# Forty-two unread matmuls in the waits of TensorE at the start of an attention and feed-forward kernel

## The chip, the core and the metric

The kernel runs on one core of one Trainium2 chip. The core has five engines that run their own queues of instructions: TensorE (PE in the profile, with its weight loads as PEld), VectorE (DVE), ScalarE (ACT), GpSimd (POOL) and SyncE (SP, which here only issues transfers). The metric is the device time of one execution in microseconds (us); less is better. The kernel before took 344.17 us, the median of three runs from 341.67 to 345.38 us.

## The reference

Eight batches of eight heads of causal attention, 576 queries each, with 16 beacon keys that every query may see; the result, as 4608 rows of 512, goes through a feed-forward layer of width 2048 with an ELU between its two products.

```python
k_all = np.concatenate([beacon_k, k], axis=2)          # B=8, H=8, S=576, D=64, 16 beacons
v_all = np.concatenate([beacon_v, v], axis=2)
scores = scale * np.matmul(q, k_all.transpose(0, 1, 3, 2))
scores = np.where(causal, -1000000000.0, scores)
a = np.exp(scores - scores.max(-1, keepdims=True)); a /= a.sum(-1, keepdims=True) + 1e-09
x = np.matmul(a, v_all)                                # -> (4608, 512)
h = x @ w_in                                           # (512, 2048)
g = np.where(h > 0.0, h, np.exp(np.minimum(h, 0.0)) - 1.0)
out = g @ w_out                                        # (2048, 512)
```

## The kernel before

The work is cut into pairs of heads: pair `n` is two heads of batch `n // 4`. For a pair of the first three batches, q and k are loaded as 32-bit floats (L261, issued by SP or ACT), cast to 16 bits (`cast_pair`, L215 when on DVE), and turned by nine plus one transposes on TensorE. For the four pairs of the first batch that is `do_T2` (L355 to L364): its ten transposes fill two tiles named `tr2`, and four copies (`do_copy2`) on ACT and DVE bring them to `kT` and `qT`. For later batches `do_T` (L351, L353) uses one tile of another kind. From batch 3 on, transfers do the turning.

`do_SC` (L402) then makes the scores of a pair in four units, each in a tile of kind `sc`, of which there are two. ACT takes the exponential of each (`do_exp`, L411), POOL zeroes what the causal mask forbids (`do_mask`, L418), and `do_AV` (L438) multiplies by v (loaded, then cast by L215) into a tile `av`. DVE divides by the row sums (L453, L454), and for the first two batches `do_xT` (L464) turns the result, which ACT or DVE copies to `xT` (L213, L215). The feed-forward layer follows by tiles of rows: the first product into `hps` (L494), the exponential on ACT (L501), a clamp on POOL (L505), the join on DVE (L512), and the second product (L569, and L561 in a form with fewer products).

The order of the work is written out by hand. Every operation has a number in `KEYS`, `plan.run` sorts all operations by it and issues them in that order, and each engine executes its own in the order issued. There are no priorities at run time: an instruction whose inputs are not ready holds up all that stand behind it on its engine.

A list `FILLS` has numbers of the same kind. For each, `plan.run` issues one call of `do_fill` (L200 to L203) at the place that the number gives in the order: a matmul of a tile of ones by itself, 128 by 256, into a tile `spare` that nothing reads. Before, there are 29 at 7.543 and two at 9.623. They stand in TensorE's queue ahead of the first pair's transposes, and between the first and the second pair's.

A tile `spare` is not a place of its own:

```python
            spare = psum.tile([P, 512], FP32, tag="ff", name="spare", bufs=4)
            nc.tensor.matmul(out=spare[:, 0:2 * P], lhsT=ones[:, 0:P], rhs=ones, start=True, stop=True)
```

`tag="ff"` with `bufs=4` is a ring of four banks of PSUM that go round in the order in which tiles are asked for, and `tr2` (two of the four for each pair), `av`, `xt` and `hps` come from the same ring. The k-th tile of the ring takes the bank of the (k-4)-th. So the matmul that writes it waits until all that wrote or read the (k-4)-th tile is done, the copies on ACT and DVE too. The list of operations keeps count of the ring for all its own work (`take=["ff"]`, `give=["ff"]`), not for `do_fill`.

Of the kernel before, what the change touches and what calls it, by code (L numbers as in the profile page):

```python
# [58 lines left out]
def kernel(  # L59
# [131 lines left out]
    with tc.tile_pool(name="psum", bufs=1, space=bass.MemoryType.PSUM) as psum:  # L191
# [406 lines left out]
        def do_store(s, m, halves):  # L598
# [11 lines left out]
        FILLS = [  # L610
            7.543, 7.543, 7.543, 7.543, 7.543, 7.543, 7.543, 7.543, 7.543, 7.543, 7.543, 7.543, 7.543, 7.543, 7.543,
            7.543, 7.543, 7.543, 7.543, 7.543, 7.543, 7.543, 7.543, 7.543, 7.543, 7.543, 7.543, 7.543, 7.543, 9.623,
            9.623,
        ]
        KEYS = [
# [483 lines left out]
```

## Time and profile before

| | |
|---|---|
| runs, median (lowest to highest) | 344.17 us (341.67 to 345.38) |
| the profiled execution's own time | 343.9 us |
| its span, first to last instruction | 342.2 us |
| TensorE busy | 326.2 us, 95% of the span |
| DVE, ACT, POOL busy | 240.5, 222.4, 191.6 us |
| transfers | 52.59 MB in 139399 packets |
| granted TensorE clock, mean | 0.989 |

The profile is of one execution. Its times count from the start of the span; the time of the execution is 1.7 us longer than the span. "Busy" of TensorE is the time with a matmul under way, which says nothing of its speed: that is in the granted clock (PEclk), 1.00 for full. In lists of instructions a row gives the start, the duration of the whole row, the engine, the line, what is written from what, and how many instructions were merged (x8); in brackets stands the idle time of the engine before it and what ended it.

### The profile page before, as it was taken

What the parts mean: (1) busy time and instruction counts of PE and PEld (TensorE: products, weight loads), DVE (VectorE), ACT (ScalarE), POOL (GpSimd) and SP (SyncE); (2) the same over time, 40 slices, a digit from 0 to 9 for tenths busy, and PEclk for the clock granted to TensorE, in tenths of its full rate; (3) what the DMA queues carried; (4) which work ended last, traced back from release to release, by engine and by line L of the source; (5) the groups of instructions that cost most, each with busy time, mean ns of one, the idle gap of its engine ahead of it and who ended that gap; (6) DMA issues with size and microseconds to landing.
All of it is one profiled execution on the core that took longest, in us unless ns stands there. A gap on an engine that the chain in (4) does not pass through costs nothing.

```text
span 342.2 us, 9215 instructions
## 1 busy us (share of the span) xinstructions
PE 326.2 (95%) x3615; PEld 225.8 (66%) x3615; DVE 240.5 (70%) x467; ACT 222.4 (65%) x347; POOL 191.6 (56%) x358
## 2 busy tenths in 40 slices
PE   7578999999999998999999999999999999999994
PEld 5356888645635674577687876675667676666684
DVE  1878879565788786766767678567776776694762
ACT  2867897877588656875577768867764663344420
POOL 4575799377658853457457475655562645434400
PEclk9969999999999999999999999999999999999999
DMA  7989999899979999999899899965604200500113
GB/s 228 250 230 243 261 244 211 162 173 186 181 145 202 213 208 152 194 203 207 152 151 227 154 140 186 214 161 123 135 0 103 62 2 12 153 32 33 61 48 108
DMA packets 139399, 52.59 MB, mean 154 GB/s; under 512 B 119388, under 2 KB 135772, under 8 KB 139356
## 3 DMA queue, kind: packets, MB, share of 16 engines
q1 hardware_dynamic: 114492, 42.11, 58.9%
q10 hardware_dynamic: 20640, 5.70, 10.3%
q0 software_dynamic: 4224, 4.19, 7.5%
q8 instruction: 28, 0.46, 0.6%
q14 instruction: 15, 0.12, 0.1%
HBM read 37.22 MB, written 9.44 MB: 136 GB/s over the span
## 4 chain that ended last, share of the span: by engine, by line
PE 75%; DMA 7%; DVE 7%; ACT 5%; POOL 2%; issue 2%; SPq 1%; ACTq 0%; DVEq 0%
PE hps L494 31%; PE ops L561 26%; PE av L438 7%; PE sc L402 7%; DMA kT<-st 4%; PE ops L569 3%; ACT et L411 3%; DVE gt L512 2%; DMA st<-in_q_dram 2%; DMA vst<-in_v_dram 2%; DVE st L215 1%; POOL e L505 1%; DVE v L215 1%; PE tr L351 1%; ACT e L501 1%
## 5 line engine op out<-in xcount | busy, mean ns | idle before, releaser
L505 POOL TENSOR_SCALAR e<-e 128x512 f32<-128x512 f32 x144 | 93.3, 654 | 94.9 <-ACT e L501 94.1
L494 PE MATMUL hps<-xT,w_in 128*128 128x512 f16 (+2 forms) x768 | 140.9, 326 | 0.7 <-DVE gt L512 0.5
L411 ACT ACTIVATE et<-sc 128x1024 f16<-128x1024 f32 (+4 forms) x128 | 109.7, 891 | 32.6 <-PE sc L402 26.7
L512 DVE SCALAR_TENSOR_TENSOR gt<-e,hps 128x512 f16<-128x512 f32 x144 | 96.3, 681 | 48.8 <-POOL e L505 48.5
L501 ACT ACTIVATE e<-hps 128x512 f32<-128x512 f32 x144 | 84.2, 600 | 48.8 <-PE hps L494 45.9
L494 PEld LDWEIGHTS <-w_in 128*128 128x128 f16 x768 | 66.0, 98 | 46.5 <-issue 5.8
L418 POOL TENSOR_SCALAR_AFFINE_SELECT et<-et 128x256 f16<-128x256 f16 (+4 forms) x160 | 69.6, 457 | 27.7 <-ACT et L411 27.4
L561 PEld LDWEIGHTS <-gt 128*128 128x128 f16 x640 | 60.9, 98 | 14.2 <-issue 1.4
L561 PE MATMUL ops<-w_out,gt 128*128 128x256 f16 x384 | 47.1, 273 | 0.0
L402 PE MATMUL sc<-qT,kT 64*128 64x80 bf16 (+3 forms) x704 | 37.7, 235 | 5.2 <-ACT et L411 2.7
L438 PEld LDWEIGHTS <-et 128*128 128x128 f16 (+1 forms) x992 | 37.4, 99 | 7.5 <-issue 1.6
L438 PE MATMUL av<-v,et 128*128 128x65 f16 (+1 forms) x992 | 40.7, 196 | 1.3 <-DVE v L215 1.3
L402 PEld LDWEIGHTS <-kT 64*128 64x128 bf16 x704 | 21.1, 97 | 23.5 <-issue 17.5
L454 DVE TENSOR_TENSOR x<-av,rl 128x256 f16<-128x256 f32 (+2 forms) x68 | 32.0, 471 | 2.5 <-DVE rl L453 0.2
L561 PE MATMUL ops<-t,gt 128*128 128x256 f16 x256 | 31.6, 273 | 0.0
L561 PEld LDWEIGHTS <-s 128*128 128x128 f16 x256 | 24.4, 98 | 5.6 <-issue 0.6
L453 DVE RECIPROCAL rl<-av 128x4 f32<-128x4 f32 (+2 forms) x68 | 12.3, 182 | 17.0 <-PE av L438 16.9
L594 DVE TENSOR_TENSOR osb<-ops,part 128x512 f32<-128x512 f32 (+1 forms) x27 | 16.9, 628 | 9.7 <-PE ops L561 6.0
L215 DVE CAST st<-st 128x1152 bf16<-128x1152 f32 (+3 forms) x19 | 15.7, 827 | 8.2 <-DMA st<-in_k_dram 3.4
L213 ACT ACTIVATE part<-ops 128x512 f32<-128x512 f32 (+1 forms) x22 | 12.2, 560 | 12.1 <-PE ops L561 12.0
L561 PE MATMUL ops<-t,s 128*128 128x256 f16 x128 | 16.1, 273 | 0.0
L569 PE MATMUL ops<-w_out,gt 128*128 128x512 f16 x64 | 16.0, 379 | 0.0
(54 smaller groups left out, 207.3 us busy)
## 6 DMA issues: line engine op xcount, KB each, us to landing
out_dram<-osb SPq DMA_DIRECT2D x32, 256.0 KB, 2.5
vst<-in_v_dram SPq DMA_DIRECT2D x18, 256.0 KB, 5.8
st<-in_q_dram SPq DMA_DIRECT2D x16, 256.0 KB, 4.4
st<-in_q_dram SPq DMA_DIRECT2D x11, 288.0 KB, 6.5
st<-in_k_dram SPq DMA_DIRECT2D x11, 288.0 KB, 6.5
st<-in_k_dram SPq DMA_DIRECT2D x9, 256.0 KB, 4.9
w_in<-in_moe_w_in_dram POOLq DMA_DIRECT2D x4, 512.0 KB, 9.6
w_out<-in_moe_w_out_dram POOLq DMA_DIRECT2D x4, 512.0 KB, 8.7
```

What stands on the lines that cost most here:

```text
L215: eng.tensor_copy(out=out, in_=in_)
L402: nc.tensor.matmul(out=sc[:, h, o:o + w], lhsT=kT[D * h:D * h + D, keys_of(n, jc)], rhs=qT[D * h:D * h + D, q0:q0 + w], start=True, stop=T ...
L411: nc.scalar.activation(out=et[:, :, 0:w], in_=scs[n, u][:, :, 0:w], func=AFT.Exp, bias=0.0, scale=float(1.0 / (D ** 0.5)))
L418: nc.gpsimd.affine_select(out=et[:, :, c0:c0 + dw], in_=et[:, :, c0:c0 + dw], compare_op=ALU.is_ge, fill=fill0, base=q0 + NB - keys.start, ...
L438: nc.tensor.matmul(out=av[:, c:c + D + 1], lhsT=ets[n, cut.unit_of[jc, at]][0:m, h, col:col + P], rhs=v16[0:m, jc, 2 * hp + h, 0:D + 1], s ...
L454: nc.vector.tensor_tensor(out=x16s[b % 2][:, blks[0]:blks[0] + nb, P * hp:P * hp + P].rearrange("q i (h d) -> q i h d", d=D), in0=av[:, :, ...
L494: nc.tensor.matmul(out=hps[:, (hi - lo) * j + a - lo:(hi - lo) * j + b - lo], lhsT=w_in16[:, cc, P * fc:P * fc + P], rhs=xT[cc][:, a % RIN ...
L501: nc.scalar.activation(out=e, in_=hpss[tt, i], func=AFT.Exp, bias=0.0, scale=1.0)
L505: nc.gpsimd.tensor_scalar(out=e, in0=e, scalar1=1.0, scalar2=0.0, op0=ALU.min, op1=ALU.max)
L512: nc.vector.scalar_tensor_tensor(out=gt, in0=e, scalar=1.0, in1=h, op0=ALU.subtract, op1=ALU.max)
L561: nc.tensor.matmul(out=bank_of(s, m, slice(half, half + 1))[:, 0], lhsT=a[:, fc, P * half:P * half + P], rhs=B_OF[m][:, fc], start=(first ...
L569: nc.tensor.matmul(out=banks[s, t4], lhsT=gts[s % 2][:, fc, P * t4:P * t4 + P], rhs=w_out16[:, fc], start=(fc == 0), stop=(fc == NFC - 1), ...
```

## The change

`FILLS` grows by 42 numbers, from 31 to 73; nothing else in the file is different. The order of every other instruction on every engine is the same as before.

```diff
         FILLS = [
             7.543, 7.543, 7.543, 7.543, 7.543, 7.543, 7.543, 7.543, 7.543, 7.543, 7.543, 7.543, 7.543, 7.543, 7.543,
             7.543, 7.543, 7.543, 7.543, 7.543, 7.543, 7.543, 7.543, 7.543, 7.543, 7.543, 7.543, 7.543, 7.543, 9.623,
-            9.623,
+            9.623, 9.623, 9.623, 9.623, 9.623, 9.623, 9.623, 9.623, 9.623, 9.623, 9.623, 9.623, 9.623, 12.503, 12.503,
+            13.230, 14.685, 15.412, 16.289, 16.289, 16.654, 16.654, 16.654, 16.654, 16.654, 16.654, 16.654, 16.654,
+            16.654, 19.025, 19.025, 19.025, 19.025, 22.600, 22.600, 22.600, 25.952, 25.952, 25.952, 25.952, 25.952,
+            28.112, 30.151,
         ]
```

In TensorE's queue the 42 stand in twelve places. By the instruction that follows them, with its start in the profile before:

| number | how many | the next instruction of TensorE |
|---|---|---|
| 9.623 | 12 more (14 in all) | transposes of the second pair (at 9.73 us before) |
| 12.503 | 2, behind the third pair's transposes | a unit of scores (12.30) |
| 13.230 | 1 | a unit of scores (13.03) |
| 14.685 | 1, behind the fourth pair's transposes | a unit of scores (14.42) |
| 15.412 | 1 | a unit of scores (15.15) |
| 16.289 | 2 | a unit of scores (16.01) |
| 16.654 | 9 | the first `av`, 16 matmuls (17.67) |
| 19.025 | 4 | scores (20.58) |
| 22.600 | 3 | scores (25.08) |
| 25.952 | 5 | transposes of a pair of the second batch (28.79) |
| 28.112, 30.151 | 1 and 1 | scores (30.96) and `xt` (33.53) |

## The prediction

> **What bounds the kernel now.** First the page's times of the engines and its slices.
>
> ```profile
> span 342.2 us, 9215 instructions
> PE 326.2 (95%) x3615; PEld 225.8 (66%) x3615; DVE 240.5 (70%) x467; ACT 222.4 (65%) x347; POOL 191.6 (56%) x358
> ...
> PEclk9969999999999999999999999999999999999999
> ```
>
> TensorE is busy for 95%, and its clock is down in the third slice alone. Two stretches of the busy times show where its idle time lies.
>
> ```profile
> 0.00:35.00 35.00, 25.83 (x350) 18.98 (x351) 23.36 (x60) 22.32 (x32) 19.95 (x45) 0.90 0.98 237
> 35.00:280.00 245.00, 242.62 (x2787) 165.62 (x2785) 177.45 (x340) 178.11 (x277) 152.97 (x281) 1.00 0.89 165
> ```
>
> In the first 35 us TensorE (second number) is idle for 35.00 - 25.83 = 9.2 us, in the next 245 us for 2.4 us. Behind the head it is the bound, so a head that ends later by x moves the end by x less 2.4 us at most; and these 2.4 us are waits for work that itself stands in the fixed order behind the head. I pass a shift on whole.
>
> The waits of TensorE in the head come next: engine and line, what it waited for, us in total, times, longest.
>
> ```profile
> PE sc L402 <- ACT et L411: 2.7, 6, 0.7
> PE tr L361 <- DVE st L215: 1.6, 1, 1.6
> PE av L438 <- DVE v L215: 1.3, 1, 1.3
> PE tr L351 <- DVE st L215: 0.8, 1, 0.8
> ```
>
> TensorE waits there for exponentials and casts: it is not the bound, and what matters is when its next *read* result comes. Last the clock (before the last two columns), in stretches of 3.41 us set by its first change at 17.11 us.
>
> ```profile
> 6.87:10.28 3.41, 1.77 (x26) 1.41 (x24) 1.37 (x3) 1.03 (x3) 1.46 (x2) 1.00 1.03 349
> 10.28:13.70 3.42, 2.50 (x37) 1.57 (x34) 2.64 (x7) 3.42 (x8) 1.56 (x2) 1.00 1.11 192
> 13.70:17.11 3.41, 1.56 (x19) 0.85 (x17) 3.41 (x5) 3.41 (x5) 3.40 (x7) 1.00 1.21 264
> 17.11:20.53 3.42, 2.04 (x24) 1.45 (x24) 3.13 (x11) 1.65 (x3) 1.44 (x3) 0.50 0.80 142
> 20.53:23.94 3.41, 3.36 (x58) 2.65 (x59) 1.70 (x6) 2.62 (x4) 3.33 (x6) 0.50 0.95 305
> 23.94:27.35 3.41, 2.76 (x58) 2.11 (x54) 2.91 (x5) 2.97 (x5) 2.71 (x5) 1.00 1.03 253
> ```
>
> The stretch with 1.56 us of TensorE is followed by half clock, that with 3.36 by full clock; 1.77 at full clock was enough to stay, 2.04 at half clock not to return. Half clock lasts 6.83 us. That is what unread matmuls can win.
>
> **The change part by part.** It adds 42 matmuls to TensorE's queue and nothing anywhere else; no transfer is issued or moved. What one costs, from the tile's row (shortest, median, longest in ns) and the two that stood behind the first pair's transposes:
>
> ```profile
> L203 PE MATMUL spare<-t x31: 272/421/421, 1.3 to 7.8; 128*128 128x256 f16 x31
> ...
> 7.71 0.38 PE L203 MATMUL spare<-t 128*128 128x256 f16 x2
> ```
>
> Two take 0.38 us and one 0.27, so the step from one to the next is 0.11 us at full clock; twice that at half. All 42 are 4.6 to 9.2 us of TensorE, which the 9.2 us of idle time would hold. But each also takes the next of the ring's four banks, and its instruction waits until the reader of the tile four back is done. Everything behind it on TensorE waits with it. So for each place the question is: when has the *last reader* of the ring's older tiles finished, and what stands behind?
>
> *First place: twelve more ahead of the second pair's transposes.*
>
> ```profile
> 9.59 0.43 DVE L215 COPY qT<-tr 128x256 bf16<-128x256 bf16 x1
> ...
> 10.06 0.49 ACT L213 ACTIVATE kT<-tr 128x256 bf16<-128x256 bf16 x2 [1.61 <-DVE qT L215]
> ...
> 9.73 0.68 PE L361 MATMUL tr<-identb,st 128*128 128x128 bf16 x9 [1.64 <-DVE st L215]
> ...
> 10.60 0.60 PE L402 MATMUL sc<-qT,kT 64*128 64x240 bf16 x8
> ...
> 11.09 1.89 ACT L411 ACTIVATE et<-sc 128x960 f16<-128x960 f32 x2
> ```
>
> Of the fourteen between the two pairs, the third needs the bank of the first pair's first `tr2` tile, and the eleventh that of its second. That tile is read last by the copies to kT on ACT, which end at 10.06 + 0.49 = 10.55; they wait for the DVE copy at 9.59, and that stands behind the very cast (8.91 to 9.67) for which the transposes wait. So the eleventh to fourteenth start at 10.6 and the transposes at 10.6 + 4 x 0.11 = 11.03, not 9.73: 1.3 us late. The scores behind them come at 11.03 + (10.24 - 9.73, the nine) + 0.06 = 11.6 instead of 10.60, and the first exponential at 12.2 instead of 11.09: **+1.1**. Nothing hides it: from 10.28 to 17.11 ACT is busy without a gap (3.42 and 3.41 us in the rows above), and the masks, casts and copies hang on these exponentials. Eight of the twelve fit into the wait; the last four cost.
>
> *The next six places, 12.503 to 16.289.* Their scores wait for the same copies or for the exponential before, so an unread matmul costs nothing, or 0.1 us at the first, and the exponentials queue on ACT anyway: 0.
>
> *Nine at 16.654, ahead of the first `av`.*
>
> ```profile
> 14.52 3.10 DVE L215 CAST v<-vst 128x512 f16<-128x512 f32 x1
> 17.54 0.88 DVE L215 COPY kT<-tr 128x256 bf16<-128x256 bf16 x3
> 18.34 0.47 DVE L215 COPY qT<-tr 128x320 bf16<-128x320 bf16 x1
> ...
> 14.55 2.79 POOL L418 TENSOR_SCALAR_AFFINE_SELECT et<-et 128x480 f16<-128x480 f16 x5
> ...
> 17.67 1.04 PE L438 MATMUL av<-v,et 128*128 128x65 f16 x16 [1.26 <-DVE v L215]
> 18.88 1.01 PE L402 MATMUL sc<-qT,kT 64*128 64x240 bf16 x8 [0.17 <-DVE st L215]
> ...
> 19.56 3.59 ACT L411 ACTIVATE et<-sc 128x960 f16<-128x960 f32 x4 [1.77 <-PE sc L402]
> ```
>
> Before, `av` ran from 17.67 beside the fourth pair's copies to kT and qT, and the scores followed 0.07 us after the qT copy (18.81). Now the first of the nine waits for that pair's kT copies and the fourth for its qT copy, so `av` cannot start before the qT copy. This ends at 18.81 + 1.1 = 19.9; six unread matmuls take 0.7; then the sixteen of `av`, which used to be covered. Was the clock at full speed up to there? From 13.70 to 17.11 the unread matmuls and the 1.1 us by which work slides in bring TensorE from 1.56 to some 2.5 us, so I take it that the clock does not fall at 17.11. From 17.11 to 20.53 there are one unit of scores (0.4), three unread (0.5) and most of the six (0.6), 1.5 us, no more than the 1.56 us on which it fell. So I take half clock from 20.53 to 23.94, half as long as before. The sixteen then take 1.04 - 0.17 (the lap of one row into the next, as 0.68 of the nine transposes against 0.51) = 0.87, the scores start at 19.9 + 0.7 + 0.87 = 21.5 instead of 18.88, and the four exponentials behind them move by **+2.6** in all, to 22.2 until 25.75.
>
> *What the clock gives back.* The fifth exponential came 1.04 us behind the fourth.
>
> ```profile
> 24.19 1.75 ACT L411 ACTIVATE et<-sc 128x800 f16<-128x800 f32 x2 [1.04 <-PE sc L402]
> ...
> 20.58 0.61 PE L402 MATMUL sc<-qT,kT 64*128 64x256 bf16 x4 [0.70 <-ACT et L411]
> ...
> 22.13 1.50 PE L438 MATMUL av<-v,et 128*128 128x65 f16 x24
> ...
> 25.53 0.64 PE L438 MATMUL av<-v,et 128*128 128x65 f16 x16
> ```
>
> It waited for the 24 matmuls of 1.50 us at half clock and the scores behind. In the new order these come after 24, at full clock: sixteen are 0.64 against 1.04, so 24 some 0.9. They are done by 25.3, the scores by 25.6, and the fifth exponential goes right behind the fourth, at 25.7 instead of 24.19: the shift falls to **+1.5**. The four at 19.025 and three at 22.600 wait for divisions that end before the exponential for which their scores wait: 0.
>
> *Five at 25.952, ahead of transposes.*
>
> ```profile
> 28.79 0.68 PE L351 MATMUL tr<-identb,st 128*128 128x128 bf16 x9 [0.82 <-DVE st L215]
> ...
> 28.57 0.39 ACT L213 ACTIVATE xT<-xt 128x256 f16<-128x256 f16 x1
> 29.94 0.97 ACT L411 ACTIVATE et<-sc 128x960 f16<-128x960 f32 x1 [0.97 <-PE sc L402]
> ```
>
> The third needs the bank that the ACT copy to xT reads until 28.57 + 0.39 = 28.96, 0.2 us later than the transposes started; with three steps of 0.11 they start at 29.3, not 28.79: **+0.5**, and the exponential at 29.94, for which ACT was idle 0.97 us, with them. The last two places wait for copies that end inside their waits: 0.
>
> **Sum**: 1.5 + 0.5 = +2.0 us; 343.9 + 2.0 = 345.9. The median of the runs is 0.3 above this execution, so I say **346.0 us**. Bounds of what the trace doesn't show: the clock in the new order (half for all of 17.11 to 23.94 keeps the +2.6, so +3.1; full throughout gives +1.4, below), and how much of the tail's 2.4 us of idle time swallows (0 to 2.4; I take 0, as its waits stand in the same order).
>
> **The clock, by rule and by row.** In this trace the clock fell after a stretch in which no wait of TensorE was over half a microsecond, but which was only 46% busy (1.56 of 3.41). The Trainium skill, page "TensorE: Matmul & The Clock Gate", section "Why this matters for your kernels", says that throughput drops when the gap between bursts is over some 3 us, one whole window of idle. By that rule the clock would not have fallen here at all, and the row speaks against it. By it there would be no half clock in the new order, the rival of full clock below, and no clock to win with the change.
>
> **The rivals.**
>
> *The clock stays full throughout (0.17).* The 1.5 us from 17.11 to 20.53 stand just at what sufficed once (1.77) and once not (1.56), and the stretches needn't lie the same in another execution. Then the sixteen take 0.64 - 0.17 = 0.47, the scores 0.2 less, the fifth exponential comes at 25.1, +0.9, and with the 0.5 the time is 343.9 + 1.4 = 345.3.
>
> *Faster: the unread matmuls fit into the waits (0.10).* If the copies were done sooner than the work behind them, only the clock would count. The prize is the 1.04 us that ACT waited before 24.19 and the 0.2 us of the first scores (0.61 against 0.40): 343.9 - 1.2 = 342.7. It decides where the eleventh of the first place starts: before 9.73 the change wins, but the copy it waits for starts at 10.06.
>
> *Slower by more: a cast of v is caught behind POOL's masks (0.20).* The cast at 14.52 took 3.10 us and ended just after POOL's row of masks (14.55 + 2.79 = 17.34); one at 19.89, with POOL idle, took 0.42.
>
> ```profile
> 19.89 0.42 DVE L215 CAST v<-vst 128x512 f16<-128x512 f32 x1
> ```
>
> The Trainium skill, page "SBUF — State Buffer", section "Who interferes with whom", has DVE and GpSimd sharing one pair of ports under an exclusive lock; the row agrees. In the new order the cast of 19.89 goes to 22.3, behind the divisions of the late `av`, and the masks of the first of the four exponentials start at 23.2. If DVE is 0.9 us later than I sum, the cast ends behind the masks and the second half of the 24 matmuls with it. The price is 1.0 (four masks, less what the exponentials hide) to 2.7 us (3.10 - 0.42): 346.9 to 348.6.
>
> *The change doesn't reach the end (0.08).* The tail's idle time and what ACT regains swallow the shift: 343.4 to 344.4.
>
> **How the numbers follow.** The forecast has 0.45, with a range of its own from 344.9 to 347.1. The range to hold 8 in 10 takes in the rivals but for the ends of the faster and the slower: 342.7 to 348.7. One per cent, 3.4 us, is about what a measurement of this kernel tells from no change (three runs lie 3.7 us apart): within it are 340.7 to 347.6. Over it lies half of the slower rival, 0.10, and 0.14 for a half clock that lasts (+3.1) and what may come on top of it; below it only a faster rival with more luck, 0.04. So faster 0.04, within 0.72, slower 0.24.
>
> **What would show it.** Right: the second pair's transposes at 11.0 and not 9.7, with an ACT copy as what ended their wait or that of an unread matmul; `av` at 20 or later, after the qT copy; no fall of the clock at 17.1; the fifth exponential hard behind the fourth; TensorE's steady stretch beginning 2 us later. Wrong: transposes at 9.7, which would mean that the ring does not bind; a cast over 2 us near 22; half clock from 17.1; or a span that grows by less than the head does.

## The result and the profile after

The changed kernel takes 348.68 us (median of 22 runs, 344.24 to 350.52) and the kernel before, on the same chip, 344.75 (22 runs, 341.15 to 347.64): a ratio of 1.0104 with a 95% interval from 1.0075 to 1.0133, so 3.6 us more by the ratio. Ratios here and below leave out slow runs, those over 1.5% above the fastest of their kernel (seven of the 22 of the change), and are not quotients of the medians shown: that quotient is 1.0114 here. The forecast was 346.0 with a range from 342.7 to 348.7, and "within 1%" as the likeliest case. The direction was right. The time stands 0.02 us inside the upper end of the range, and its 3.6 us are 1.6 more than the forecast's sum of +2.0; the ratio is just past the border between "within 1%" and "slower", with its interval on both sides.

The profiled execution took 347.3 us, 3.4 more than that of before. Its engines and clock on the page:

```profile
PE 332.0 (96%) x3657; PEld 229.3 (66%) x3657; DVE 242.4 (70%) x467; ACT 222.4 (64%) x347; POOL 192.2 (56%) x358
...
PEclk9969999999999999999999999999999999999999
```

TensorE is busy 5.8 us longer, with 42 more matmuls; the clock is still down in the third slice. The waits of TensorE from 7 to 35 us (engine and line, what it waited for; us in total, times, longest):

```profile
PE spare L203 <- DVE kT L215: 2.8, 1, 2.8
PE spare L203 <- DVE xT L215: 0.9, 1, 0.9
PE tr L351 <- ACT et L411: 0.7, 1, 0.7
PE spare L203 <- ACT qT L213: 0.4, 1, 0.4
```

Before, it was read matmuls that waited, for casts and exponentials. Now three of the four longest waits are those of unread ones, each for a *copy out of a bank of the ring* (a bank is one of the pieces of PSUM that the ring hands out). Their places in TensorE's list (start, duration, what; in brackets the idle time before and what ended it):

```profile
8.70 1.75 PE L203 MATMUL spare<-t 128*128 128x256 f16 x12 [0.40 <-ACT qT L213]
10.28 0.67 PE L361 MATMUL tr<-identb,st 128*128 128x128 bf16 x9
...
19.53 2.23 PE L203 MATMUL spare<-t 128*128 128x256 f16 x9 [2.79 <-DVE kT L215]
21.56 1.08 PE L438 MATMUL av<-v,et 128*128 128x65 f16 x16
22.57 1.01 PE L402 MATMUL sc<-qT,kT 64*128 64x240 bf16 x8
...
32.22 1.03 PE L203 MATMUL spare<-t 128*128 128x256 f16 x5 [0.90 <-DVE xT L215]
33.09 0.66 PE L351 MATMUL tr<-identb,st 128*128 128x128 bf16 x9
```

The first `av` starts at 21.56 (17.67 before), the scores behind it at 22.57 (18.88), the transposes behind the five at 33.09 (28.79). How DVE and POOL stood just before that:

```profile
15.17 3.90 DVE L215 CAST v<-vst 128x512 f16<-128x512 f32 x1 [0.23 <-DMA vst<-in_v_dram]
18.99 0.88 DVE L215 COPY kT<-tr 128x256 bf16<-128x256 bf16 x3
19.80 0.48 DVE L215 COPY qT<-tr 128x320 bf16<-128x320 bf16 x1
...
14.32 3.34 POOL L418 TENSOR_SCALAR_AFFINE_SELECT et<-et 128x480 f16<-128x480 f16 x6
17.62 0.60 POOL L215 CAST v<-vst 128x512 f16<-128x512 f32 x1
18.18 0.61 POOL L418 TENSOR_SCALAR_AFFINE_SELECT et<-et 128x512 f16<-128x512 f16 x1
```

And ACT, where the exponentials of the fourth pair and those behind it now stand in one row of seven:

```profile
23.26 6.21 ACT L411 ACTIVATE et<-sc 128x960 f16<-128x960 f32 x7 [5.13 <-PE sc L402]
```

The clock, in stretches of 3.41 us as before (TensorE's busy time is the second number, its clock the third from the end):

```profile
14.10:17.52 3.42, 2.14 (x22) 1.03 (x20) 3.19 (x5) 3.42 (x5) 3.41 (x7) 1.00 1.21 223
17.52:20.93 3.41, 1.40 (x7) 0.81 (x7) 2.81 (x6) 0.60 (x1) 1.27 (x3) 0.50 0.67 112
20.93:24.34 3.41, 3.41 (x32) 2.23 (x30) 1.46 (x5) 1.08 (x2) 0.04 (x1) 0.50 0.70 212
```

The clock fell behind a stretch with 2.14 us of TensorE and stayed down for these two stretches, 6.83 us, as long as before.

To see where the time comes in, each read matmul of one trace is paired with the same one of the kernel before, in order; the difference of their starts is the *shift*. Worked out so for the change:

| us in the profile before | 9.7 | 14.4 | 17.7 | 25.1 | 29.2 | 87.7 | 100 | 136 | 172 | end |
|---|---|---|---|---|---|---|---|---|---|---|
| shift, us | +0.55 | +0.23 | +3.89 | +2.66 | +4.28 | +4.28 | +3.59 | +3.09 | +3.70 | +3.42 |

All of it is there by 29 us. At 88 us it is the same to a hundredth, and it moves only later, by up to 1.4 us at a step.

### The profile page after: what moved, and what is told of

Read it like the earlier page. It is cut to its first block, busy times and chain, and to the rows that moved or that the text cites. A ratio compares the mean times of both kernels' runs of the same rounds, so it can differ in the third digit from the quotient of the medians.

```text
span 345.6 us, 9297 instructions
## 1 busy us (share of the span) xinstructions
PE 332.0 (96%) x3657; PEld 229.3 (66%) x3657; DVE 242.4 (70%) x467; ACT 222.4 (64%) x347; POOL 192.2 (56%) x358
## 4 chain that ended last, share of the span: by engine, by line
PE 80%; DVE 7%; DMA 6%; ACT 2%; POOL 2%; issue 1%; SPq 1%; DVEq 0%; ACTq 0%
PE hps L494 32%; PE ops L561 26%; PE av L438 8%; PE sc L402 7%; PE ops L569 4%; DMA vst<-in_v_dram 3%; DMA st<-in_k_dram 2%; ACT et L411 2%; DVE gt L512 2%; DVE v L215 1%; PE tr L351 1%; POOL e L505 1%; PE spare L203 1%; DVE st L215 1%; DMA out_dram<-osb 1%
## 5 line engine op out<-in xcount | busy, mean ns | idle before, releaser
L505 POOL TENSOR_SCALAR e<-e 128x512 f32<-128x512 f32 x144 | 94.6, 663 | 94.3 <-ACT e L501 93.3
L438 PE MATMUL av<-v,et 128*128 128x65 f16 (+1 forms) x992 | 40.0, 194 | 0.0
L594 DVE TENSOR_TENSOR osb<-ops,part 128x512 f32<-128x512 f32 (+1 forms) x27 | 16.9, 628 | 9.1 <-PE ops L561 7.2
L215 DVE CAST st<-st 128x1152 bf16<-128x1152 f32 (+3 forms) x19 | 16.4, 864 | 6.7 <-DMA st<-in_q_dram 6.1
L203 PE MATMUL spare<-t 128*128 128x256 f16 x73 | 15.3, 353 | 5.6 <-DVE kT L215 2.8
```

The lines of the kernel that those rows point to most:

```text
L215: eng.tensor_copy(out=out, in_=in_)
L438: nc.tensor.matmul(out=av[:, c:c + D + 1], lhsT=ets[n, cut.unit_of[jc, at]][0:m, h, col:col + P], rhs=v16[0:m, jc, 2 * hp + h, 0:D + 1], s ...
L505: nc.gpsimd.tensor_scalar(out=e, in0=e, scalar1=1.0, scalar2=0.0, op0=ALU.min, op1=ALU.max)
```

## The experiments

The theory: (a) waits of unread matmuls for readers of the ring hold up the read work behind them; (b) the first cast of v on DVE, caught behind POOL's masks, adds to it. The rivals: the 42 cost by being there (TensorE's time, or the clock), or the place of the head's end costs by what it does to the transfers behind.

| run | edit to the kernel before | median, us | ratio to before (95%) | shift at 14 / 29 / 88 us / end, in its profile |
|---|---|---|---|---|
| the change | 42 unread | 348.68 | 1.0104 (1.0075 to 1.0133) | +0.23 / +4.28 / +4.28 / +3.42 |
| one_bank | 42, one tile per place | 346.10 | 1.0054 (1.0022 to 1.0087) | +1.08 / +0.11 / +0.16 / +1.60 |
| first12 | the 12 at 9.623 | 349.66 | 1.0144 (1.0097 to 1.0191) | +1.03 / +2.84 / +2.89 / +7.18 |
| nine | the 9 at 16.654 | 349.89 | 1.0180 (1.0120 to 1.0240) | +0.28 / +3.38 / +3.38 / +5.16 |
| five | the 5 at 25.952 | 347.59 | 1.0075 (1.0030 to 1.0119) | -0.62 / +2.15 / +2.16 / +1.46 |
| rest | the 16 others | 348.16 | 1.0086 (1.0046 to 1.0127) | -0.37 / +0.21 / +0.33 / +2.00 |
| first6 | 6 at 9.623 | 348.44 | 1.0097 (1.0058 to 1.0137) | +0.17 / +1.37 / +1.37 / +2.97 |
| end16 | 16 behind the last read matmul | 345.23 | 1.0000 (0.9969 to 1.0032) | -0.27 / +0.87 / +0.87 / +0.19 |
| v_pool | first cast of v on POOL | 343.64 | 0.9971 (0.9943 to 1.0000) | -0.33 / -2.15 / -2.14 / -1.83 |
| v_pool_42 | that, and all 42 | 345.24 | 1.0024 (0.9990 to 1.0058) | +1.43 / +0.93 / +0.94 / +4.61 |
| v_pool_nine | that, and the 9 | 346.16 | 1.0036 (1.0003 to 1.0069) | -0.65 / -1.73 / -1.67 / +0.48 |
| v_pool_rest | that, and the 16 | 345.50 | 1.0021 (0.9988 to 1.0053) | -0.38 / -1.62 / -1.46 / +1.48 |
| v_pool_one_bank | that, and 37 (without the five), one tile per place | 344.30 | 0.9989 (0.9955 to 1.0022) | +0.46 / -1.07 / -0.34 / +1.38 |

Each ratio is to the kernel before on the same chip, from 6 runs of first12 and nine, 10 of five, rest, v_pool_42 and v_pool_one_bank and 12 of the others. The shifts are of one execution each, which need not be a typical one: those of v_pool_42 (348.49) and first12 (351.25) were the longest of their kernels, those of v_pool (342.13) and v_pool_nine (344.43) the shortest.

### One tile of the ring per place

```diff
+            if op is not None and op.eng == "PE":
+                self.spare = None
             fn()
...
-            spare = psum.tile([P, 512], FP32, tag="ff", name="spare", bufs=4)
+            if getattr(plan, "spare", None) is None:
+                plan.spare = psum.tile([P, 512], FP32, tag="ff", name="spare", bufs=4)
+            spare = plan.spare
```

On top of the change, unread matmuls that follow each other write the same tile, so that a place takes one bank, however many stand there (lines are four higher in this profile).

> All 42 stay where they are, but the unread matmuls of one place write one tile together, so a place takes one bank of the ring and not up to fourteen. If the ring's waits are the cause (theory), the second pair's transposes no longer wait for the first pair's copies, av starts when its cast is done, and the time goes back to 344.7 or below, down to 1.2 us below if the clock stays up. If the unread matmuls cost by themselves, by their time on TensorE or by what they do to the clock (rival), it stays near the 348.7 of the changed kernel.

Measured: 1.0054, about half of the loss and between the two expectations; the interval (1.0022 to 1.0087) overlaps that of the change (1.0075 to 1.0133). In TensorE's list, and below it DVE:

```profile
17.35 1.16 PE L207 MATMUL spare<-t 128*128 128x256 f16 x9
18.34 0.65 PE L442 MATMUL av<-v,et 128*128 128x65 f16 x16
...
28.37 0.71 PE L207 MATMUL spare<-t 128*128 128x256 f16 x5 [0.89 <-DVE xT L219]
...
15.84 0.84 DVE L219 CAST v<-vst 128x512 f16<-128x512 f32 x1
```

The nine run without a wait, `av` starts at 18.34 instead of 21.56, and the shift falls to -1.23 at 25 us: TensorE is ahead of the kernel before. The five still wait, and it is back at +0.11 by 29 us. The nine no longer wait for banks, as (a) says. But this run changed a second thing: the first cast of v took 0.84 us here, not 3.90, and ended at 16.68 instead of 19.07. With the cast of the change, `av`, which needs it, could not have started before 19.1; so, as an estimate, 2.5 of the 3.2 us that `av` gained are the banks' and 0.7 the cast's. Whether the cast is short because of the edit or in this execution alone, one profile does not tell. And the time is still 0.5% over before, with next to no shift in this profile's head.

### The parts alone: twelve, nine and five

```diff
-            9.623,
+            9.623, 9.623, 9.623, 9.623, 9.623, 9.623, 9.623, 9.623, 9.623, 9.623, 9.623, 9.623, 9.623,
```

> Only the twelve more ahead of the second pair's transposes. Theory: transposes 1.3 us late, the first exponential 1.1 us late, the end +1.1, 345.9. If the shift is swallowed later in the head: below +0.4.

```profile
10.55 0.60 PE L203 MATMUL spare<-t 128*128 128x256 f16 x4 [1.73 <-ACT kT L213]
10.99 0.67 PE L361 MATMUL tr<-identb,st 128*128 128x128 bf16 x9
```

The last four wait for ACT's copy to kT and the transposes start at 10.99, where the prediction had 10.6 and 11.03. The shift is +1.03 up to 14.4 us, as expected. The time is not: 1.0144 is some 5 us, against +1.1. In this profile the shift grows to +2.18 at the first `av`, because the first cast of v took 4.25 us, and by another 4.3 us behind 88 us; the waits of the twelve explain only the first step.

```diff
-            9.623,
+            9.623, 16.654, 16.654, 16.654, 16.654, 16.654, 16.654, 16.654, 16.654, 16.654,
```

> Only the nine ahead of the first av. Theory: av stands behind the fourth pair's qT copy, the scores are late by 1.6 (full clock) to 2.6 us (half), of which the clock gives back up to 1.1; the end +0.5 to +2.6. Rival (each unread matmul costs its share, 9 of 42): +0.8 with av where it was, at 17.7.

```profile
16.62 0.39 PE L203 MATMUL spare<-t 128*128 128x256 f16 x2
19.49 0.27 PE L203 MATMUL spare<-t 128*128 128x256 f16 x1 [2.47 <-DVE kT L215]
20.29 1.16 PE L203 MATMUL spare<-t 128*128 128x256 f16 x6 [0.53 <-DVE st L215]
21.24 1.09 PE L438 MATMUL av<-v,et 128*128 128x65 f16 x16
```

Here the two steps are apart: two matmuls pass, the third waits for the copies to kT, the last six start when DVE is done with the qT copy (it ended at 20.24; the wait is put down to a small cast behind it), and `av` is last. Alone, the nine leave +3.38 in the head. That is more than the expected +0.5 to +2.6, and so is the time, 1.0180 or some 6 us.

```diff
-            9.623,
+            9.623, 25.952, 25.952, 25.952, 25.952, 25.952,
```

> Only the five ahead of a transpose of the second batch. Ring theory: they wait for two copies to xT that end behind the cast for which the transposes wait, so these are 0.5 us (the sum of the prediction) to 1.1 us (as in the changed kernel's profile) late, and the end +0.5 to +1.1. If the head has slack there: 0.

```profile
30.09 1.03 PE L203 MATMUL spare<-t 128*128 128x256 f16 x5 [1.05 <-ACT xT L213]
30.95 0.66 PE L351 MATMUL tr<-identb,st 128*128 128x128 bf16 x9
...
28.73 0.75 DVE L215 CAST st<-st 128x1152 bf16<-128x1152 f32 x1
29.65 0.39 ACT L213 ACTIVATE xT<-xt 128x256 f16<-128x256 f16 x1
```

The cast that the transposes need is done at 29.48, and they start at 30.95: 1.5 us late, three times what was predicted. The wait is for the predicted copy (29.65 + 0.39 = 30.04), but the five take 1.03 us, where those that share a bank take 0.71. The time, 1.0075 or 2.6 us, is also over the expected +0.5 to +1.1.

The three parts and the 16 others cost 1.44 + 1.80 + 0.75 + 0.86 = 4.85% alone and 1.04% together. Part of that is plain: a delay at one place hides the wait at the next. But the nine alone come out above all of them together (1.0120 to 1.0240 against 1.0075 to 1.0133, intervals that overlap), and no sum of waits in the head gives that: their profile's head is 0.9 us ahead of that of the change.

### What should cost nothing: the 16 others, six at the first place, 16 at the end

```diff
-            9.623,
+            9.623, 12.503, 12.503, 13.230, 14.685, 15.412, 16.289, 16.289, 19.025, 19.025, 19.025, 19.025, 22.600, 22.600, 22.600,
+            28.112, 30.151,
```

> The sixteen others: without the twelve, the nine and the five. Ring theory: none of them has to wait for a reader that the work behind doesn't wait for too, so the time of before, within 0.3 per cent. Rival (each unread matmul costs its share of the +3.9 us): +1.5. The profile's row for the first cast of v on DVE says in passing whether its 3.1 us of before is what it usually is, or the 3.9 to 4.25 us of three kernels since; nothing ahead of it is changed enough to matter.

Measured 1.0086, which is not the nothing that the prediction gave these places. In its profile, TensorE, and below it DVE:

```profile
18.95 0.65 PE L438 MATMUL av<-v,et 128*128 128x65 f16 x16 [2.81 <-DVE kT L215]
...
14.80 3.69 DVE L215 CAST v<-vst 128x512 f16<-128x512 f32 x1 [0.45 <-DMA vst<-in_v_dram]
18.41 0.88 DVE L215 COPY kT<-tr 128x256 bf16<-128x256 bf16 x3
```

The cast of v is done at 18.49, and `av` still waits until 18.95, by the profile for a copy to kT: seven more unread tiles stand ahead of it than before, the ring is turned by them, and now a *read* tile has the busy bank. That is 0.46 us. The head is at +0.21 by 29 us all the same; the rest of the loss comes behind it.

```diff
-            9.623,
+            9.623, 9.623, 9.623, 9.623, 9.623, 9.623, 9.623,
```

> Six more ahead of the second pair's transposes and not twelve: eight in all, so that neither an unread matmul nor the transposes take the bank that the ACT copy to kT reads. Ring theory: the transposes start when their cast is done, and the end is that of before, within 0.3 per cent, against +1.4 per cent with twelve. If the loss goes by the number of unread matmuls: half of it, +0.7 per cent.

Six at the first place wait for no copy that ends late, and the transposes are on time (shift +0.17 up to 14.4 us). Yet it measured 1.0097. Its first cast of v:

```profile
14.70 4.22 DVE L215 CAST v<-vst 128x512 f16<-128x512 f32 x1
```

It took 1.1 us longer than in before's profile, which with its start 0.18 later is all of the +1.30 at 17.7 us. That (a) is the only cause is ruled out by the time: these six wait for no late copy and cost 0.97%. That the six made the cast longer is not shown. In five, whose instructions up to 25 us are those of before, it took as long:

```profile
13.90 4.24 DVE L215 CAST v<-vst 128x512 f16<-128x512 f32 x1
```

```diff
-            9.623,
+            9.623, 340.000, 340.000, 340.000, 340.000, 340.000, 340.000, 340.000, 340.000, 340.000, 340.000, 340.000, 340.000, 340.000,
+            340.000, 340.000,
```

> A control: sixteen unread matmuls, as many as in the run of the sixteen others, behind the last read matmul of the kernel, where nothing waits for them. If what those sixteen cost (+0.86 per cent) comes from their places in the head (theory), this is the time of before, within 0.3 per cent. If any further instructions on TensorE cost (rival: their mere number, or how the program is laid out), +0.5 per cent or more. Its head is that of before, so its profile is a second look at the 3.10 us of the first cast of v: near 3.1 if that was usual, near 4.2 if not.

Measured 1.0000. A longer program and more work for TensorE at the end cost nothing; it is the place in the head that does. Its head is that of before, so this profile shows before's head in a second execution:

```profile
15.43 3.06 DVE L215 CAST v<-vst 128x512 f16<-128x512 f32 x1 [1.07 <-DMA vst<-in_v_dram]
...
13.74 3.33 POOL L418 TENSOR_SCALAR_AFFINE_SELECT et<-et 128x480 f16<-128x480 f16 x6
17.04 0.60 POOL L215 CAST v<-vst 128x512 f16<-128x512 f32 x1
```

The same order of work ends this cast at 18.49 (and at 18.14 in five), against 17.62 in before's profile. There POOL had stopped for a tenth of a microsecond behind its six masks:

```profile
14.00 3.33 POOL L418 TENSOR_SCALAR_AFFINE_SELECT et<-et 128x480 f16<-128x480 f16 x6
17.44 0.65 POOL L215 CAST v<-vst 128x512 f16<-128x512 f32 x1
```

DVE's cast ended 0.3 us after that gap opened (17.33 to 17.44). Where POOL has no gap, as here and in the change, DVE's cast ends only beside POOL's own cast and one more mask. So some 0.9 us of the head seem to turn on a tenth, in the kernel before too, and the profile of before that all shifts count from is the one with the early end.

### The first cast of v on POOL

```diff
-            "SDSPSDSDSDAPASDADAADADSADAADDDDDSSDADDDAADSSDDDDDDDDDSPDDDPDPDADDDADDDDDDADDSPSPSASPAASASSDADSSDAASS"
+            "SPSPSDSDSDAPASDADAADADSADAADDDDDSSDADDDAADSSDDDDDDDDDSPDDDPDPDADDDADDDDDDADDSPSPSASPAASASSDADSSDAASS"
```

The second letter of this string gives the first cast of v to POOL (P) instead of DVE (D).

> The kernel before with one cast moved: the first cast of v, which took 3.1 us on DVE behind the masks, is made by POOL between its masks. If that cast holds up the chain of the head, the fourth pair's copies end 2 to 3 us earlier and the time falls by 1 to 2 us, to 343; if the chain has another path of the same length, no change beyond 0.4 us.

```profile
14.82 0.61 POOL L215 CAST v<-vst 128x512 f16<-128x512 f32 x1
...
14.20 0.88 DVE L215 COPY kT<-tr 128x256 bf16<-128x256 bf16 x3
...
16.02 0.66 PE L438 MATMUL av<-v,et 128*128 128x65 f16 x16
```

On POOL the cast takes 0.61 us in its turn. DVE's copies come 3.3 us sooner, `av` at 16.02 instead of 17.67, and the head of this profile is 2.15 us shorter. The time is 0.9971 of before (interval to 1.0000), the best of all kernels here: 1.0 us, the lower edge of the 1 to 2 us expected.

On top of it came the lists shown above: all 42, the nine, the 16, and the 42 without the five in the form with one tile per place.

> The changed kernel, with the first cast of v on POOL. If the wait of that cast on DVE makes a large part of the loss, because the kT and qT copies for which the unread matmuls wait stand behind it, the nine find the qT copy done at 15.5 and cost almost nothing: the loss against before falls to that of the twelve and the five, less the 1.0 that the move itself wins, 344.5 to 346. If the ring costs the same wherever the cast is: 348.7 - 1.0 = 347.7.

> The nine ahead of the first av, with the first cast of v on POOL. They wait for the fourth pair's qT copy as before, but it then ends at 15.5 us instead of 19 to 20, and av has no more to wait for than its own masks. Theory: the nine cost 0 to 1.0 us against v_pool, so 343.6 to 344.6, and not +1.8 per cent as without the move. Rival (the ring's wait costs the same wherever the cast is): 343.6 + 5 = 348.6.

> The sixteen others with the first cast of v on POOL. If they lose only by what they do to that cast's wait on DVE, the time is that of v_pool, 343.6 (0.997 of before). If they lose 3 us wherever the cast is: 346.6.

> No wait of the ring's is left that the work behind doesn't have: one tile for each place, without the five, and the first cast of v on POOL. What is left is the clock: if it stays up from 17 us on, scores and av of half clock (1.5 us in v_pool's profile) are won: 342 to 343. If unread matmuls cost by themselves: no better than v_pool, 343.6, or worse.

Against v_pool, the 42 now cost 1.0024 / 0.9971 = 1.0053 (1.001 to 1.010, from the two intervals), the nine 1.0065, the 16 1.0050, and 37 with one tile per place 1.0018. (By the medians these prices would be 0.05% to 0.5%.) Only the 42 came out where they were expected; the nine, the 16 and the 37 all took longer. The nine in v_pool_nine:

```profile
15.70 1.16 PE L203 MATMUL spare<-t 128*128 128x256 f16 x9
16.69 0.65 PE L438 MATMUL av<-v,et 128*128 128x65 f16 x16
```

They wait for nothing: DVE's last copy from their banks ended at 15.16. So (b) holds for the nine: without that cast on DVE their price falls from 1.80% to 0.65%, with intervals that lie apart. What works is less that the unread matmuls lengthen the cast than that the copies they wait for stand behind it. For the 42 the price falls from 1.04% to 0.53%, with intervals that still overlap. The clock as a cause falls: in the page of v_pool_42 it is

```profile
PEclk9999999999999999999999999999999999999999
```

full throughout, as in the heads of the other three, while v_pool itself has one stretch at half clock. What unread matmuls could win was won there, and did not show in the time.

In the profile of v_pool_rest the *second* cast of v was caught instead:

```profile
17.61 3.66 DVE L215 CAST v<-vst 128x512 f16<-128x512 f32 x1
```

which lifted the shift from -2.43 to -1.30 at 25 us. It is the place that the prediction's rival named, in another kernel.

### Behind the head

In v_pool_rest the shift goes from -1.46 at 88 us to -0.02 at 100 and +1.84 at 124; the last step, 1.6 us at 122, stands behind a wait for DVE's write to the output tile (L594), and what delayed that was not followed. The issues on SP (the instructions that start transfers) near 88 us, in v_pool and then in v_pool_rest:

```profile
87.17 2.52 SPq L300 DMA_TRANSPOSE kT<-st  x2
```

```profile
89.10 4.39 SPq L300 DMA_TRANSPOSE kT<-st  x2
```

Two transposing transfers take 2.52 us to issue in one and 4.39 in the other, and what stands behind them on SP is later by as much. Of the 80 such transfers in an execution, 6 to 14 take over 1.6 us to issue instead of 1.2 in the fourteen profiles, 12 in before and 13 after; which ones differs from profile to profile. ACT's queue shows another kind of delay around two loads of v that it issues, in before and in v_pool_42:

```profile
175.06 1.93 ACTq L328 DMA_DIRECT2D vst<-in_v_dram  x2
```

```profile
176.29 5.81 ACTq L328 DMA_DIRECT2D vst<-in_v_dram  x2
182.20 0.81 ACT L411 ACTIVATE et<-sc 128x768 f16<-128x768 f32 x1 [5.32 <-DMA kT<-st]
```

In v_pool_42 the two issues themselves take 0.41 and 0.39 us; the 5.0 us between them are a wait, which the profile puts down to a transposing transfer to kT. The exponential behind them comes 5.1 us later than that of before (177.09), and the shift of v_pool_42 jumps there from +1.23 to +5.11. In the other profiles it is 1.3 to 2.5 us from the start of the first issue to the end of the second.

The change itself loses part of its shift at such a place:

```profile
130.80 0.45 PE L402 MATMUL sc<-qT,kT 64*128 64x128 bf16 x6 [1.26 <-DMA kT<-st]
```

This is the kernel before: TensorE waits 1.26 us for a transposing transfer. In the change the same scores start at 133.91 without a wait, and the shift falls from +4.53 to +3.10.

So what a head leaves is changed later by how long transfers take to issue or to land, by a microsecond or more; what that depends on was not tried. Whether unread matmuls in the head make this worse on average, or whether these are single draws, was not tried: no run moved the transfers alone. The ratios of first6, rest and the four kernels with unread matmuls and the cast on POOL leave 0.2 to 1.0%, mostly some 0.5%, over their counterparts, of which the waits for banks in their heads explain only a part. **The cause of that remainder stays open.**

## Why the prediction was right, and where it was not

*What bounds the kernel*: right up to 88 us, where the shift of 29 us is unchanged. "I pass a shift on whole" held to 0.9 us at the end of the change; the wait at 130.80 us was not one "for work that itself stands in the fixed order behind the head" but for a transfer, and it took in 1.4 us of the shift. In other kernels the same stretch moved it by up to 4.3 us.

*First place, +1.1 by the eleventh to fourteenth waiting until 10.55*: right as a mechanism, and first12 shows it to 0.05 us. The rule given ahead of the prediction, that the k-th tile of the ring takes the bank of the (k-4)-th, does not hold as it stands: by it the fourth of the fourteen would wait for the second `tr2` tile, and in first12 it is the eleventh, as the prediction has it. A bank that is still to be read is passed over, as far as these rows tell. In the changed kernel the same transposes start at 10.28, because the cast ahead of them (its load landed 0.7 us sooner in that execution) was early; that is luck. "Eight of the twelve fit into the wait" was read as if eight could be added for nothing; six were, by the transposes' start, and they still cost 0.97% (first6).

*Six places at 0*: wrong. With their banks shifted, the first `av` waits for a copy to kT (0.46 us in rest); the prediction followed the banks of the unread tiles and not those of the read tiles that come behind them.

*Nine, "`av` cannot start before the qT copy"*: right in kind. It was sized at 20.6 for `av` and 21.5 for the scores; measured 21.56 and 22.57. Two terms were mis-sized. The cast of v was left at 3.10 and took 3.90; that is a term the trace of before could not give, as unchanged heads have it end 0.5 (five) and 0.9 us (end16) later too. And "I take it that the clock does not fall at 17.11" failed: the stretch ahead held 2.14 us of TensorE, not far from the 2.5 assumed, and the clock fell all the same, for two stretches and not one. The nine and `av` ran wholly at half clock, so that 1.28 us lie between the end of the qT copy (20.28) and `av`, where 0.7 was taken.

*What the clock gives back*: right. The fifth exponential stands hard behind the fourth, and the shift drops from +3.89 to +2.66, by 1.2 where 1.1 was predicted.

*Five, +0.5*: mis-sized. The shift goes from +2.66 to +4.28, 1.6 us; alone, the transposes start 1.5 us after their cast. The kind of wait was named rightly, a copy to xT, but its time had moved with the work, and it is the first of the five that waits and not the third: in five they start at 30.09, 30.41, 30.52, 30.74 and 30.85, so the transposes come 0.86 us after the first, where three steps of 0.11 were counted.

*The rivals*: "faster, the unread matmuls fit into the waits" did not come, and one_bank shows what it would need: there, with a cast of v that took 0.84 us, TensorE was 1.2 us ahead at 25 us, until the five. "Slower by more: a cast of v is caught behind POOL's masks" did not come at the cast that it named (0.42 us in the change). The first cast, caught in before already, took the 0.8 us above longer; heads that nothing was added to show the same, so it is not shown that the unread matmuls did it. Moving that cast brings the loss from 1.04% to 0.53%. The Trainium skill, page "SBUF — State Buffer", section "Who interferes with whom", says that DVE and GpSimd share one pair of ports under an exclusive lock; the casts of 3.06 to 4.25 us beside POOL's masks against one of 0.42 agree. "Full clock throughout" did not come in the change; where it came, with the cast on POOL, it won no time that can be measured. "The change doesn't reach the end" came for 0.9 us of it.

Put together, from the rows: +2.0, less 0.4 (the cast of v starts at 15.17, when its load has landed, 0.65 late and not 1.1), +0.8 (the cast), +0.7 (half clock: 0.6 at the nine and 0.1 at `av`), +1.1 (the five), less 0.9 behind the head, is +3.3; the two profiles differ by 3.4. The 0.4, the 0.8 and the 0.9 hang on when loads, a cast and a transfer fell in these two executions. So the kind of wait and the direction were foreseen; that the time still fell inside the range, by 0.02 us, is luck, with three terms too small by 2.6 us together and two that happened to make up for 1.3.

## What to carry to other kernels

A matmul that nothing reads is free only if the bank it writes is free: give such fillers a bank of their own, or one tile per place, and look at the last reader of the bank before counting idle TensorE time as room. They also turn a shared ring, so follow the banks of the *read* tiles behind them. Before filling a wait for the clock's sake, look at what ends that wait; here, moving one cast of v to the engine whose row of masks it was stuck behind gave 0.3% (interval to 0), and the full clock nothing that could be measured.

## What the runs showed of the hardware that was not expected

The clock fell behind a stretch of 3.41 us in which TensorE was busy for 2.14 us, 63%; before, it had stayed full behind one of 1.77. How full the stretch must be, or of what, these runs do not tell. Half clock lasted 6.83 us in before and in the change, and 10.24 us in five and end16, whose instructions up to there are those of before.

A DVE cast that takes 0.42 us with POOL idle took 3.1 to 4.25 us beside POOL's back-to-back masks in eight of the nine profiles that have it there, and 0.84 in the ninth (one_bank); in before it ended 0.3 us after a gap of 0.10 us on POOL opened. The issue of one transposing transfer on SP takes 1.2 us as a rule and 1.6 to 3.3 us about once in seven.
